# An mLSTM layer and a spectral mixer on one core: the gates of chunk 1 computed apart from those of chunks 2 to 5, and a new order of the steps

## The chip, the cores and the metric

The kernel runs on one core of a Trainium2 chip. Its time is the device time of one execution in microseconds; several executions are timed, and the median counts. TensorE is called PE here (its weight loads PEld), VectorE DVE, ScalarE ACT, GpSimd POOL; SP is the engine whose queue issues nearly all DMAs.

## The reference

Two layers follow one another. The first is an mLSTM: for 4 batches of 8 heads a 40x40 state is updated token by token over 768 tokens, with gates that are kept stable by a running maximum.

```
for t in range(768):
    m_new = max(f[t] + m, i[t])
    C = exp(f[t] + m - m_new) * C + exp(i[t] - m_new) * outer(v[t], k[t])
    n = exp(f[t] + m - m_new) * n + exp(i[t] - m_new) * k[t]
    y[t] = sigmoid(o[t]) * (C @ q[t]) / max(abs(n . q[t]), 1)
    m = m_new
```

The second takes y as x (4 x 768 tokens x 320 channels):

```
theta = x @ w_theta
y = w_tok_r @ (x * cos(theta)) + w_tok_i @ (x * sin(theta))     # over the tokens
u = x + y
out = u + max(u @ w_ch, 0)
```

## The kernel before

**Chunks, units, pairs.** The 768 tokens are cut into six chunks (0 to 5) of 128. A *unit* is one chunk of one batch, so there are 24 units, n = 4 * chunk + batch; units 0 to 3 belong to chunk 0, 4 to 7 to chunk 1. Two units make a *pair*, and the mixer works on pairs: pair 0 is units 0 and 1, pair 1 units 2 and 3, pair 2 units 4 and 5.

**The gates** (gate_part, L186 to L245). The gates of all heads lie in one tile, a row per head, the tokens along it. A scan on DVE gives the running maximum (best, L196). decay (L199 to L207) turns it into the sum of log decays inside each chunk, one scan for each chunk, and a DMA (L177) stores it to g_d in DRAM. POOL subtracts (L215), growth (L210, L211) makes the weights of the inputs, an exponential on ACT (L222) follows, and PE turns the result chunk by chunk (turn, L228), which ACT or DVE copies to bwT (L231). For chunks past 0, leave (L241) and one more exponential (L243) give the decay from the start of a chunk, stored to e_d (L177). In the kernel before this is done once for chunk 0 and once for chunks 1 to 5 together, that is on 640 columns.

**A unit** (unit_loads and attention). SP loads queries and keys (qk, L313), tokens (tok_t, L317), and, from chunk 1 on, two things that the gates stored: dt from g_d, spread over 128 partitions (L322), and eb from e_d in three DMAs (L330), behind the queries q_t (L327). PE makes the scores (L370); ACT takes the exponentials *exps* (L389, eight pieces); POOL's *select* (L393) clears what lies in the future; DVE *weighs* the scores (L399); PE multiplies by the values, *pv* (L406 with the state, L410 without). From chunk 1 on DVE or POOL first *scales the queries* by eb (L484). A denominator (L417 to L424), an output gate (L430, L432) and X (L439) end the unit. *fade* (L444 to L449), *state* (L454), fadeC (L460, L462) and *update* (L468 to L475) carry the state on.

**A pair** (mix_part and mix). PE transposes X (L609); x_hi, x_lo (L621, L625) split it in two parts of fewer bits, and x_acc (L631, L633) adds it to the sums; PE makes *theta* (L647); turns, part and abs (L655 to L671) bring the angle into range; two *sines* on ACT (L674, L675); *times* (L684) multiplies by x; z_hi and z_lo (L687, L690) split the product. Then five *mixing steps* j = 0 to 4 on PE (L549, 12 products each), each gathered by DVE or ACT (L563 to L570). Pair 0 goes through mix_part in two halves, one for each unit.

**Weights.** The token weights of a chunk come in three pieces. SP loads a piece into one of two raw buffers (L773); size, upper, *lower* and hi, lo (L263 to L285) split it. The load of a piece can go out when the lower of the piece two before it is done (wpool has two raw buffers).

**The order.** Every step is added to a plan by `add`, with its engine and its dependences, and gets the next number. The string ORDER then lists all steps in the order in which they are issued, a number and an engine letter each (V is DVE, A is ACT, G is POOL, T is PE, D is a DMA on SP). Each engine and SP's queue follow that order strictly; between engines the waits come from the data. Some steps at the end of the numbering are *fillers* (L870 to L880): with T they run two products of ones on PE, with V they do nothing.

```
t = self.waiting[n]
assert n not in done and eng in (t.alts or t.eng)
t.eng = eng
t.fn()
```

## Time and profile before

| | |
|---|---|
| median of 3 executions | 355.92 us (355.57 to 356.24) |
| the profiled execution's own time | 357.73 us |
| its span, first to last instruction | 356.0 us |
| granted TensorE clock, mean | 0.947 |
| moved by DMA | 61.56 MB in 25164 packets |
| table loads on ACT | 27 of 1.28 us |

The profile is of one execution. It has a page with the busy time of each engine, a coarse picture of the span and the chain of work that ended last, followed back from the end, and answers to questions on the trace: the timeline of an engine, the waits by engine, the busy time in chosen stretches of the span. A timeline row has start and length in us, engine, line of the kernel, operation, output and inputs, the number of instructions merged into it, and in square brackets the idle time of the engine before it with what ended it. PE's steps overlap a little at their ends, so rows of the timeline add up to slightly more than the time that they take in a row.

### The profile page before, as it was taken

The numbers are of one execution on the slowest core, as the hardware profiler recorded it, in microseconds if no ns is written. First come the engines' busy times: TensorE is split into PE (matmuls) and PEld (weight loads), VectorE is DVE, ScalarE is ACT, GpSimd is POOL, SyncE is SP. The second block draws the span as 40 slices with busy tenths as digits, with TensorE's granted clock in tenths as the row PEclk, the third lists the DMA queues.
The fourth block names the chain that finished last, engine by engine and source line by source line (L and its number), as shares of the span: only waits on it lengthen the run. The fifth ranks groups of instructions, "written<-read, shape, count | busy, mean of one in ns | idle before, by whom it ended". The sixth has DMA issues, their size and how long they took to land.

```text
span 356.0 us, 6570 instructions
## 1 busy us (share of the span) xinstructions
PE 325.5 (91%) x2286; PEld 303.9 (85%) x2289; DVE 297.3 (84%) x629; ACT 220.5 (62%) x567; POOL 123.1 (35%) x111
## 2 busy tenths in 40 slices
PE   1487969979899999998999999999999999999995
PEld 1366959859799999997999989999999989998885
DVE  4998699786889998999989998798899998658632
ACT  2989788888979979596585838987850412201000
POOL 1223442323434636247352611614330092702000
PEclk9877676978999999999899999999999999999999
DMA  6965792996886764489627286346630021000155
GB/s 228 395 228 172 226 261 57 302 327 214 244 329 215 243 210 134 152 250 323 203 71 257 79 263 238 121 142 193 228 87 0 2 43 33 1 2 0 46 196 202
DMA packets 25164, 61.56 MB, mean 173 GB/s; under 512 B 3204, under 2 KB 11052, under 8 KB 25132
## 3 DMA queue, kind: packets, MB, share of 16 engines
q1 hardware_dynamic: 23915, 59.84, 51.1%
q0 software_dynamic: 1216, 1.31, 2.0%
q8 instruction: 18, 0.29, 0.3%
q14 instruction: 15, 0.11, 0.1%
HBM read 55.71 MB, written 4.12 MB: 168 GB/s over the span
## 4 chain that ended last, share of the span: by engine, by line
PE 63%; DVE 17%; DMA 12%; ACT 3%; POOL 2%; issue 2%; SPq 2%; DVEq 0%; POOLq 0%
PE pm L549 25%; PE pm L955 10%; PE pm L647 9%; PE ph L410 8%; DMA qk<-in_qk 5%; DMA eb<-e_d 4%; PE sc L370 3%; PE ph L406 3%; DVE acc L563 2%; PE pm L454 2%; DVE dt L399 2%; DMA q_t<-in_q 2%; DMA sg<-in_og 1%; DVE val L271 1%; DVE val L275 1%
## 5 line engine op out<-in xcount | busy, mean ns | idle before, releaser
L549 PE MATMUL pm<-w,z 128*128 128x384 f32 x600 | 112.2, 339 | 0.0
L549 PEld LDWEIGHTS pm<-w,z 128*128 128x128 f32 x600 | 103.4, 188 | 1.4 <-DVE acc L563 0.2
L563 DVE TENSOR_TENSOR acc<-pm,acc 128x384 f32<-128x384 f32 x100 | 52.1, 549 | 10.9 <-PE pm L549 10.6
L389 ACT ACTIVATE dt<-dt,bwT 128x128 f32<-128x128 f32 x160 | 49.0, 391 | 7.7 <-DMA dt<-g_d 7.6
L410 PE MATMUL ph<-tok_t,dt 128*128 128x41 f32 x384 | 49.4, 291 | 0.0
L410 PEld LDWEIGHTS ph<-tok_t,dt 128*128 128x128 f32 x384 | 48.5, 205 | 0.7 <-issue 0.2
L393 POOL TENSOR_SCALAR_AFFINE_SELECT dt<-dt 128x1024 f32<-128x1024 f32 (+1 forms) x26 | 29.3, 1130 | 49.6 <-ACT dt L389 37.5
L647 PE MATMUL pm<-wthp,xs 128*128 128x320 f32 (+1 forms) x216 | 38.3, 352 | 3.2 <-DVE xs L625 3.2
L647 PEld LDWEIGHTS pm<-wthp,xs 128*128 128x128 f32 (+1 forms) x216 | 30.7, 206 | 8.7 <-issue 4.8
L399 DVE TENSOR_TENSOR dt<-sc,dt 128x512 f32<-128x512 f32 x44 | 28.1, 680 | 1.4 <-PE sc L370 1.3
L955 PE MATMUL pm<-u,w 128*128 128x384 f32 (+1 forms) x112 | 28.4, 355 | 0.0
L370 PE MATMUL sc<-qk 64*128 64x128 f32 x352 | 26.5, 292 | 1.8 <-DMA qk<-in_qk 1.8
L370 PEld LDWEIGHTS sc<-qk 64*128 64x128 f32 x352 | 22.2, 193 | 5.2 <-issue 1.6
L690 POOL TENSOR_TENSOR z<-ab,z 128x640 fp32r<-128x640 f32 x8 | 12.8, 1603 | 35.8 <-DVE den L423 21.4
L549 PE MATMUL pm<-wsm,z 128*128 128x384 f32 x120 | 24.6, 359 | 0.0
L967 DVE SCALAR_TENSOR_TENSOR acc<-pm,acc 128x384 f32<-128x384 f32 x20 | 10.8, 555 | 14.5 <-PE pm L955 14.5
L549 PEld LDWEIGHTS pm<-wsm,z 128*128 128x128 f32 x120 | 22.2, 201 | 0.2
L406 PE MATMUL ph<-C,q_t 120*128 120x123 f32 x120 | 17.2, 279 | 5.2 <-DVE X L439 2.7
L406 PEld LDWEIGHTS ph<-C,q_t 120*128 120x128 f32 x120 | 15.4, 191 | 6.8 <-POOL q_t L484 3.0
L955 PEld LDWEIGHTS pm<-u,w 128*128 128x128 f32 (+1 forms) x112 | 17.6, 187 | 3.0 <-issue 3.0
L430 ACT ACTIVATE sg<-sg,den 128x40 f32<-128x40 f32 x72 | 16.7, 314 | 5.0 <-DVE den L424 5.0
L922 ACT CAST u<-acc 128x768 fp32r<-128x768 f32 x4 | 3.2, 834 | 26.4 <-DVE acc L563 21.5
(136 smaller groups left out, 603.8 us busy)
## 6 DMA issues: line engine op xcount, KB each, us to landing
qk<-in_qk SPq DMA_DIRECT2D x24, 512.0 KB
dt<-g_d SPq DMA_DIRECT2D x20, 512.0 KB
raw<-in_wtok SPq DMA_DIRECT2D x18, 512.0 KB
tok_t<-in_tok SPq DMA_DIRECT2D x24, 364.5 KB
sg<-in_og SPq DMA_DIRECT2D x12, 320.0 KB
q_t<-in_q SPq DMA_DIRECT2D x20, 180.0 KB
eb<-e_d SPq DMA_DIRECT2D x60, 60.0 KB
out<-acc SPq DMA_DIRECT2D x5, 384.0 KB
```

Of the source, the lines that this page charges most:

```text
L370: nc.tensor.matmul(u.sc[s][:, hp], u.qk[rows, 1, hp], u.qk[rows, 0, hp], start=True, stop=True)
L389: nc.scalar.activation(u.dt[:, h, :], src, AF.Exp, bias=bwT[:, c, r:r + 1])
L393: nc.gpsimd.affine_select(d, d, pattern=[[0, h1 - h0], [1, P]], compare_op=ALU.is_ge, fill=0.0, base=0, channel_multiplier=-1)
L399: nc.vector.tensor_mul(d2[:, s], u.sc[s], d2[:, s])
L406: nc.tensor.matmul(u.ph[:, gg * 3 * E1:(gg + 1) * 3 * E1], u.q3[:, gg, :], C[b][:, gg, :], start=(gg == 0), stop=False)
L410: nc.tensor.matmul(u.ph[:, h * E1:(h + 1) * E1], u.dt[:, i, :], v1(h, h + 1), start=(c == 0 and i == 0), stop=(i == H - 1))
L430: nc.scalar.mul(u.s3[:, h], u.s3[:, h], u.den[:, h])
L549: nc.tensor.matmul(pm[:, :TH], x.z[:, a, s, j * P:(j + 1) * P], w[x.c][:, b, s, th * TH:(th + 1) * TH], start=(k == 0), stop=(k == last))
L563: nc.vector.tensor_add(a, pm[:, :TH], a)
L647: nc.tensor.matmul(S_.th[b - b0][:, :DM], p.xs[a0:a1, a, k, :], wt5[a0:a1, s, k, :], start=(x == of(b)[0]), stop=(x == of(b)[-1]))
L690: ENG[e].tensor_sub(zv(1, s), trig(s), zv(0, s).bitcast(F32))
L955: nc.tensor.matmul(o.pm[jj][:, :TH], E_.w[s][a0:a1, col:col + P], us[pr, k][a0:a1, a, ts], start=(x == ones[jj][0]), stop=(x == ones[jj][-1]))
```

## The change

gate_part is called twice for the later chunks: once for chunk 1 alone, once for chunks 2 to 5. The second call's scan starts from the end of the first's. Each has its own store to g_d and e_d (the rows of those tensors are now sliced), its own turn and copies, and its own exponentials. unit_loads of a unit now waits for the stores of its own chunk. The list `gone`, which says when the gates' tile may be used for the weights of chunk 2, holds the stores and turns of both calls. The second call has 11 steps, and so has the first, where one call had 13; so there are 9 steps more, and 3 fillers.

All numbers in ORDER from 78 on are therefore 9 higher for the same step as before (12 higher for the last ones, from the fillers on): 114T is theta of the first half of pair 0 and was 105T. 56 to 66 are chunk 1's gates (56 best, 58 decay, 59 store to g_d, 62 turn, 66 store to e_d), 67 to 77 those of chunks 2 to 5 (69 decay, 70 store, 73 turn, 77 store). Other steps, in the new numbers: 144T the mixing step j=1 of pair 0; 118A and 133A the sines of pair 0's halves, 123A the second z_hi and 124V the z_lo behind it; 242V the last lower of chunk 1's weights, 385D the raw load that follows from it, 266D the loads of q_t and eb for unit 5; 268G and 271V unit 5's scaling of the queries and weighing, 272T its pv; 318G unit 6's scaling, 395A and 396G the hi and lo of the last piece of chunk 2's weights, 338G the select of unit 7; 161A the sigmoid of chunk 1's output gates (before, 152A); 319A and 337A the exps of units 6 and 7.

The order is new as a whole, and for many steps so is the engine: DVE, ACT and POOL have 447, 189 and 99 steps before and 437, 199 and 105 after, counting fillers as none. On POOL stand 11 scalings of the queries instead of 7, and 13 times instead of 9. The last call on PE (the channel product of pair 1's middle columns) is the same, and so is the number of products of each kind, except for 8 fillers on PE instead of 5.

```
--- before.py
+++ after.py
@@ -45,55 +45,55 @@
 ORDER = """
-0V 960G 1D 6D 17D 21D 2D 18D 19D 9D 10V 4D 12V 151D 7D 11G 8D 26A 13V 25D 27V 20D 14A 154D 24D 15T 28V 155T 56V 29A
-30A 32A 31V 16A 22T 156A 33V 58V 38A 69A 71A 81A 34V 59D 39V 23T 35A 36A 70G 98A 37V 966T 153D 40V 82T 73V 72G 43A 48D
-5A 57G 75V 986T 976T 44V 152A 84T 41A 74T 60V 3A 85A 158T 42V 76T 83V 157G 99T 49A 169D 66V 77A 87A 78V 45V 165A 89T
-159V 79G 218D 86G 80V 168D 170T 61A 88G 90V 100V 55G 91T 92V 171A 50V 93T 101T 238D 166T 94A 95V 102A 236D 64T 51V 46A
-62T 96V 52A 104V 47G 67A 103V 63A 68D 998V 105T 53V 65A 237D 219A 224D 962V 167V 172G 242A 97V 106V 116T 54G 107V 160T
-117V 220V 108A 109A 173T 256D 161V 221V 162V 222A 230D 110V 239D 163A 118V 113G 174V 120T 223G 255D 225A 164V 111A
-243G 175T 121V 180A 122V 980V 226V 240T 123A 231A 112V 124A 983T 227V 181T 176A 114A 232V 228A 305D 119A 370D 250A
-254D 177V 115V 125V 135T 178V 260A 306D 182V 128G 179V 241V 183T 129V 244V 229G 233V 245T 371A 130V 184A 376D 372V
-257D 186A 138A 251T 137A 234A 185V 261G 258T 126A 246V 136V 310A 324D 247V 323D 127V 131T 373V 235V 382D 304D 248A
-259V 322D 147T 262V 318G 311G 374A 249V 133A 252A 263T 268V 963V 148V 375G 377A 132V 253V 134A 149A 378V 307D 150A
-383A 187T 264A 328A 390D 384V 269T 188A 379V 308T 265V 270A 522D 189V 329G 985T 380A 312V 388D 190A 143T 309G 302D
-191A 266V 381G 267V 271V 313T 385V 523A 192V 394A 524V 326T 408D 139T 314V 406D 525V 325D 315V 330V 395G 316A 389D
-528D 144V 392T 140V 526V 193A 195V 145A 319T 194G 146A 396V 196A 272T 407D 142A 534D 410T 386A 456D 197V 141A 273A
-988V 320V 214T 327V 412A 317V 387G 275V 321V 527G 331T 529A 215V 391D 274V 336A 530V 276T 458D 338A 474D 332V 999V
-216V 989V 971V 333V 217A 531V 334G 337T 277A 393G 198T 335V 535A 457D 339V 413G 462A 278V 409D 536V 397T 532A 964V
-279V 303A 974V 414V 463G 202T 476D 402G 674D 199V 200V 398V 201V 280A 411V 206T 399V 537V 204V 400G 203V 205V 460T
-404A 281V 968V 284V 282A 210T 540D 208V 283G 454D 285A 992V 997V 464V 209A 680D 480A 403T 286V 478T 207V 533G 405V
-401V 340T 459D 212V 415T 538V 211V 213V 675A 481G 341V 420A 990V 343V 539G 293T 342V 542D 416A 558D 676V 344T 482V
-417V 1010V 294V 418G 546A 295V 544T 345V 290T 677V 461V 686D 678A 475D 346V 547G 422A 419V 421T 681A 679G 291V 347A
...
+0V 969G 1D 21D 17D 6D 2D 18D 8D 19D 10V 9D 12V 24D 7D 20D 11G 4D 13V 25D 56V 14A 58V 67V 59D 26A 15T 164T 27V 32A 57G
+28V 33V 29A 30A 16A 22T 31V 60V 38A 34V 90A 35V 93T 39V 36A 78A 37V 91T 40V 94A 69V 48D 43A 41A 80A 107A 23T 44V 70D
+96A 64V 45V 165A 108T 42V 227D 162D 81G 79G 92A 68G 82V 49A 98T 3A 50V 83T 46A 84V 166G 47V 85T 51V 228A 71V 52A 233D
+163D 109A 167T 178D 229V 86A 5A 177D 61A 87V 982T 230V 88A 979T 168V 95G 239D 995T 97G 231A 99V 55G 65A 179T 101V 72A
+174A 89V 53G 100T 75V 180A 232V 54G 110T 102T 189A 111V 113V 62T 76A 975T 103V 247D 112V 246D 234A 104V 66D 1001T 240A
+160D 105G 73T 245D 181G 114T 74V 63V 106V 235V 125T 115A 169T 116V 126A 236V 251A 259V 379D 175T 77D 117V 988V 170V
+127V 265D 182T 171V 237A 264D 252G 118A 190T 183V 238G 129T 172A 119G 249T 130V 122G 191V 998T 131V 176A 173V 241V
+380A 184T 248D 132A 133A 263D 381V 120A 128A 123A 1010T 185A 269A 315D 974T 134V 242V 121V 385D 124V 314D 266D 186V
+144T 382V 187V 383A 391D 250V 243A 188V 384G 135A 253V 147A 192T 319A 260T 277G 146V 254T 137V 981V 193V 270G 138A
+161A 194V 244G 145V 267T 255V 333D 256V 313D 136V 140T 386A 139V 195A 257V 271V 268G 261A 156T 320G 392A 1027V 262V
+143A 258V 142A 316D 337A 387V 272T 331D 141V 388V 393V 531D 317T 332D 389A 273A 327A 196T 989V 274V 394V 157V 390G
+537D 158V 159A 397D 321V 395A 399D 275A 396G 278T 1005V 991V 197V 152T 338G 1031V 198V 279A 276V 318G 199A 280V 335T
+155A 532V 538A 978V 154V 322T 970V 533V 200A 415D 398D 539V 148T 403A 417D 334D 534V 153V 201G 339V 311D 281T 543D
+328T 149V 204G 282A 150V 151V 401T 202A 283V 323A 329A 345G 999V 284V 285T 205A 203V 421A 206V 1019V 1038V 324V 223T
+325V 286A 336V 326V 422G 330V 340T 404G 224V 400D 980V 287V 225A 535A 288A 540V 465D 536V 541A 219T 226A 467D 1030V
+347V 683D 289A 544V 416D 341V 405V 346T 1012V 342V 207T 402V 312A 343V 290V 344V 293G 419T 983V 986V 1023V 220V 209V
+221A 348V 406T 294A 1014V 545V 418D 222A 210A 471A 411V 211T 546V 485D 463D 208V 407V 408V 483D 291V 466D 409V 215T
+689D 295V 547A 413A 976V 212V 292G 423V 214A 213A 412T 420V 349T 484D 997V 410V 472G 469T 414V 350A 542G 218V 217A
+424T 489A 216V 990V 1007V 1036V 473V 429G 684V 352V 490G 302T 551D 351V 468D 479G 1020V 984V 425V 426V 353T 549D 548V
+427A 685V 430T 690V 354A 304V 487T 303V 972V 1008V 1028V 431A 355V 299T 567D 432V 356A 555A 994V 996V 470V 486D 428V
...
@@ -211,12 +211,13 @@
             nc.vector.tensor_add(by(bw[64:P]), by(bw[64:P]), by_G(G[64:P])[:, :, P - 1:P].broadcast_to([64, n, P]))
 
         a = add("V", us, prio, best, [loaded, after])
+        gated.append(len(plan.waiting) - 1)
         warm_after.append(a)
         j = add("G", 2 * us, prio, lambda gi=i_: nc.gpsimd.tensor_sub(gi, gi, m[:, up]), [a])
         a = add("V", 0.3 * n + 2 * us + 0.45 + 0.2 * (c0 > 0), prio, decay, [a])
         decayed = a
         if c0:
-            decayed = load(0.25, prio, lambda: g_d.rearrange("c r t -> r c t"), by_G(G[0:NR]), [a])
+            decayed = load(0.25, prio, lambda: g_d[c0 - 1:c1 - 1].rearrange("c r t -> r c t"), by_G(G[0:NR]), [a])
         w = add("V", 2 * us, prio, growth, [a, j])
         warm_after.extend([a, w])
         x = add("A", us, prio, lambda: nc.scalar.activation(bw[64:P, t], bw[64:P, t], AF.Exp), [w], "exp")
@@ -241,7 +242,7 @@
                 nc.vector.tensor_add(by(E), by_G(G), gs[:, c0:c1].broadcast_to([P, n, P]))
             e = add("V", us, prio, leave, [w])
             e = add("A", us, prio, lambda: nc.scalar.activation(E[:, t], E[:, t], AF.Exp), [e], "exp")
-            return decayed, done, load(0.25 if c0 else 0.05, prio, lambda: e_d.rearrange("c r t -> r c t"), by(E[0:NR]), [e])
+            return decayed, done, load(0.25 if c0 else 0.05, prio, lambda: e_d[c0 - 1:c1 - 1].rearrange("c r t -> r c t"), by(E[0:NR]), [e])
         return a, done
 
 
@@ -249,7 +250,7 @@
 
     halves = []
 
-    warm_after = []
+    gated, warm_after = [], []
 
     def split(hi, lo, raw, n, prio, loaded, after=(), scale=None):
 
@@ -832,9 +833,13 @@
 
     turned, stored = {0: turned0}, {}
 
-    stored[1], done, stored[2] = gate_part(1, NC, 2000 + PAR["grest"], l_gr, A0)
-    for k in range(1, NC):
-        turned[k] = done
+    prior = A0
+    for c0, c1 in ((1, 2), (2, NC)):
+        g_stored, done, e_stored = gate_part(c0, c1, 2000 + PAR["grest"] + c0, l_gr, prior)
+        prior = plan.waiting[gated[-1]]
+        gone.extend([g_stored, *done, e_stored])
+        for k in range(c0, c1):
+            turned[k], stored[k] = done, (g_stored, None, e_stored)
     for x in GROUPS[0][1:]:
         for k in range(3):
             mix_weights(x, k)
@@ -845,13 +850,11 @@
                 for k in range(3):
                     mix_weights(x, k)
         if n > 1:
-            unit_loads(n, () if c == 0 else (stored[1], None, stored[2]),
+            unit_loads(n, () if c == 0 else stored[c],
                        NOW + PAR["du2"] if n == 2 else 1000 * n + PAR["load"])
         attention(n, turned[c], signed[n // 4])
         if n % 2:
             mixer(q)
-        if n == 3:
-            gone.extend([stored[1], *turned[1], stored[2]])
         if n % 4 == 1 and n // 4 < NC - 1:
             k = n // 4 + 1
```

More of the change, by code (lines that the diff above doesn't have):

```diff
@@ L63 @@
-279V 303A 974V 414V 463G 202T 476D 402G 674D 199V 200V 398V 201V 280A 411V 206T 399V 537V 204V 400G 203V 205V 460T
-404A 281V 968V 284V 282A 210T 540D 208V 283G 454D 285A 992V 997V 464V 209A 680D 480A 403T 286V 478T 207V 533G 405V
-401V 340T 459D 212V 415T 538V 211V 213V 675A 481G 341V 420A 990V 343V 539G 293T 342V 542D 416A 558D 676V 344T 482V
-417V 1010V 294V 418G 546A 295V 544T 345V 290T 677V 461V 686D 678A 475D 346V 547G 422A 419V 421T 681A 679G 291V 347A
-299T 292V 348A 682V 424T 301V 465T 470V 488A 548V 349G 300V 352G 423V 425A 562T 466V 687A 477D 426V 472A 287T 683V
@@ new lines @@
+689D 295V 547A 413A 976V 212V 292G 423V 214A 213A 412T 420V 349T 484D 997V 410V 472G 469T 414V 350A 542G 218V 217A
+424T 489A 216V 990V 1007V 1036V 473V 429G 684V 352V 490G 302T 551D 351V 468D 479G 1020V 984V 425V 426V 353T 549D 548V
+427A 685V 430T 690V 354A 304V 487T 303V 972V 1008V 1028V 431A 355V 299T 567D 432V 356A 555A 994V 996V 470V 486D 428V
+308T 686V 301V 687A 300V 556G 357A 491V 433T 474T 691V 358V 480T 1015V 310V 361G 569D 359A 553T 695D 1003V 309V 475A
+476V 296T 362A 985V 557V 488G 434A 477G 481A 435V 571T 360G 436V 1016V 1025V 437T 363V 297V 688G 1029V 478V 482V 497G
@@ new lines @@
+492T 298V 438A 552D 971V 1021V 696V 697V 550D 568D 376T 499A 439V 493V 1004V 698V 440A 494V 498T 441A 1024V 1013V 495V
+370T 554V 618D 699A 617D 496V 442G 573A 619D 1000V 1037V 973V 378V 615D 500V 558T 377V 570D 692V 445V 835D 841D 443V
+367T 446V 559A 563A 992V 372V 574G 371V 565G 305T 464A 369V 444G 368V 564T 560V 575V 700G 581A 373T 566V 447G 306V
+693A 620D 621T 307V 623A 572G 375V 374V 637D 501T 1002V 694V 635D 364T 636D 561V 504V 562V 502A 624G 576T 503V 836A
+365V 1032V 837V 505T 577A 641A 703D 701D 625V 578V 842A 838V 639T 506A 366V 579G 847D 582T 642G 580V 454T 507V 702D
@@ new lines @@
+622G 719D 643V 508A 583A 843V 626T 509A 631V 584V 457T 627A 455V 707A 638D 510V 633V 721D 632T 844V 705T 456V 513G
+634V 839A 460T 459V 649A 704D 708G 977V 458V 840G 709V 769D 448T 514A 511A 1035V 1011V 462V 515G 461V 725A 1022V 1039V
+585T 628V 449V 706G 723T 450V 586A 512G 451T 715A 587V 588V 640G 589T 848V 1009V 629V 726G 630V 1033V 453V 1018V 452V
+849V 644T 590A 591V 850V 522T 592A 771D 651V 787D 645A 593A 646V 647V 650T 767D 524V 525T 523V 720D 648V 594V 597V
+595A 710T 652V 596G 598A 616A 527V 722D 526V 599V 653T 993V 727V 528T 711A 717A 1026V 712V 654A 713G 716T 775A 789D
@@ new lines @@
+770D 714V 773T 724V 718V 728T 655V 656V 776G 793A 609T 735V 855D 772D 529V 729V 530V 851A 777V 794G 657T 853D 788D
+1043D 730V 610V 783G 611V 733V 791T 658A 774G 734T 845A 867D 659V 612T 731V 660A 732V 661A 795V 778T 736V 1006V 613V
+790D 859A 662G 600T 779V 869D 614V 663V 780V 665V 737T 784T 601V 860G 666A 602V 857T 738A 781V 785A 740V 792G 606T
+801A 739V 664G 861V 741T 667G 873A 608V 782V 786V 768A 796T 607V 856D 742A 519T 797V 913D 1034V 798V 911D 743V 854D
+799G 744V 516T 874G 521V 745A 800V 520V 858G 805T 803G 517V 871T 806V 746G 1017V 518V 802T 807V 680T 749G 808V 747V
@@ new lines @@
+750A 875V 809T 917A 751G 681V 804V 748G 862T 810V 846G 682V 987V 852V 603T 863A 927D 811V 870D 812V 813A 668T 914D
+604V 864V 605V 865G 1049D 868D 677T 912D 918G 931A 669V 926D 925D 866V 670V 671T 678V 679V 814V 674T 815A 673V 672V
+872V 817V 876T 1042A 675V 818V 1044A 676V 1045V 758T 877A 928D 878V 816V 879G 761T 759V 1046V 760V 1047A 1055D 880V
+1048G 915T 763V 916G 762V 881T 930V 755T 919V 932G 882A 819V 920T 884V 1050V 883V 929T 921V 757V 756V 885T 922V 933V
+923A 1056A 820T 924V 886A 1051V 1040V 887V 934T 888V 1057V 889A 1058V 826T 935V 821V 1052V 1059A 822V 890G 764T 827V
@@ new lines @@
+893G 891A 828V 823T 936V 894A 765V 892G 1053A 766V 937A 895G 752T 824V 825V 938V 1060V 939T 753V 754V 940A 1041V 1054V
+902T 942V 1062G 941V 896T 903V 904V 899T 898V 897V 1063V 1064G 905T 901V 900V 1061G 908T 906V 907V 1065V 943T 1067V
+1069A 910V 1066G 909V 1071A 829T 1068V 944A 945V 1072V 946A 832T 947A 1070V 831V 1091T 834V 948V 830V 949V 1089T 951V
+1092V 952A 833V 953G 1084T 950G 954T 1085V 1090V 1086V 963T 955V 956V 957T 965V 964V 1073T 958V 1094V 959V 1096V 1097G
+960T 1075V 1074V 1095V 966T 962V 961V 1098V 1099G 1076T 968V 967V 1100V 1102A 1101V 1081T 1078V 1103G 1077V 1080D
@@ L97 @@
+1109T 1083V 1082V 1088D 1079D 1127T 1111V 1110V 1113D 1093D 1112D 1119T 1128V 1104T 1120V 1121V 1122D 1123D 1114T
+1105V 1106V 1107D 1129D 1108D 1087D 1124T 1116V 1115V 1118D 1117D 1125V 1126D
 """.split()
```

29 lines of the change are left out of this document (removed).

## The prediction

> **What bounds the kernel now.** I read the page first: busy time of the engines, then the chain of waits by engine.
>
> ```profile
> PE 325.5 (91%) x2286; PEld 303.9 (85%) x2289; DVE 297.3 (84%) x629; ACT 220.5 (62%) x567; POOL 123.1 (35%) x111
> PE 63%; DVE 17%; DMA 12%; ACT 3%; POOL 2%; issue 2%; SPq 2%; DVEq 0%; POOLq 0%
> ```
>
> PE carries most of the chain that ended last, but 91% is an average over stages, so I cut the span at places where PE's work changes: the first product of the mixing (59.4), a wait (71.7), its end and what follows (84.4), the third call of theta (105.3), the last transposes (288.4). The columns are busy us of PE, PEld, DVE, ACT and POOL with instructions in brackets, then granted clock, DMA share and GB/s.
>
> ```profile
> 0.00:59.40 59.40, 40.05 (x269) 35.20 (x271) 48.62 (x95) 46.74 (x137) 19.07 (x24) 0.77 0.71 228
> 59.40:71.70 12.30, 11.71 (x88) 10.84 (x86) 9.96 (x24) 11.27 (x36) 3.45 (x3) 1.00 0.90 266
> 71.70:84.40 12.70, 10.13 (x63) 9.17 (x64) 8.63 (x22) 9.77 (x29) 3.80 (x4) 0.73 0.80 275
> 84.40:105.30 20.90, 19.61 (x160) 17.83 (x161) 19.10 (x44) 19.21 (x54) 6.96 (x6) 1.00 0.81 271
> 105.30:288.40 183.10, 180.59 (x1343) 172.51 (x1343) 170.14 (x376) 126.69 (x306) 73.58 (x61) 0.99 0.52 169
> ```
>
> From 105.3 on PE idles 2.5 us in 183 and runs at the full clock: PE's own work is the bound there, with DVE close behind (170.14 of 183.10). Before 59.4 PE idles 19.4 us and its clock is 0.77: there DVE and ACT, not PE, decide when the next product may start. Between, PE is nearly always occupied, yet at a lower clock for a while. So a new order can win only ahead of 105.3; behind it, it can chiefly add waits.
>
> **What PE loses between 59.4 and 105.3.** The chain of waits, at the full clock, gives a price for each kind of PE step: theta, score, a mixing step, state, transposes, and the two halves of pv.
>
> ```profile
> 125.40 2.59 PE pm L647 x18
> 127.99 1.09 PE sc L370 x16
> 129.08 2.28 PE pm L549 x12
> 131.36 0.63 PE pm L454 x6
> 134.09 0.55 PE pm L609 x5
> 134.64 0.67 PE ph L406 x6
> 135.30 1.72 PE ph L410 x16
> ```
>
> ```profile
> 59.39 2.33 PE L549 MATMUL pm<-w,z 128*128 128x384 f32 x12
> 74.27 0.90 PE L406 MATMUL ph<-C,q_t 120*128 120x123 f32 x6 [2.67 <-DVE X L439]
> 77.11 4.94 PE L647 MATMUL pm<-wthp,xs 128*128 128x320 f32 x18
> 96.50 1.16 PE L370 MATMUL sc<-qk 64*128 64x128 f32 x16 [1.28 <-DMA qk<-in_qk]
> 105.12 0.80 PE L454 MATMUL pm<-tok_t 128*120 128x123 f32 x6
> 165.97 0.93 PE L406 MATMUL ph<-C,q_t 120*128 120x123 f32 x6 [1.76 <-POOL q_t L484]
> 168.44 3.90 PE L549 MATMUL pm<-wsm,z 128*128 128x384 f32 x12
> ```
>
> From 59.39 to 105.12 stand 6 mixing steps, 4 pv, 5 scores, 2 theta, 3 state and 2 transposes. Rounding a mixing step to 2.2 (the chain's shorter ones are near 2.1): 13.2 + 9.6 + 5.45 + 5.2 + 1.9 + 1.1 = 36.4 us of work in 45.7 us, so 9.3 us are lost. 2.67 and 1.28 are waits; theta at 77.11 took 4.94 where 2.59 is the price, at the half clock that follows the wait. The rest is short waits, the half clock of two neighbours, and steps slightly over price (about 1.3, which I leave in both kernels).
>
> **Part 1: where the first mixing step comes (A).** In the new list, as in the old, step j=1 of pair 0 waits for the second z_hi on ACT and the z_lo on DVE behind it. In the old trace ACT does 40 steps from the first size of chunk 0's weights to that z_hi:
>
> ```profile
> 13.11 0.71 ACT L263 ACTIVATE val<-raw 128x512 f32<-128x512 f32 x1
> 18.78 0.60 ACT L283 ACTIVATE val<-val 128x480 f32<-128x480 f32 x1 [0.96 <-DVE val L275]
> 26.92 1.28 ACT L389 ACT_TABLE_LOAD   x1
> 28.21 1.14 ACT L389 ACTIVATE dt<-pm,bwT 128x128 f32<-128x128 f32 x4
> 42.11 2.44 ACT L389 ACTIVATE dt<-dt,bwT 128x128 f32<-128x128 f32 x8
> 50.80 2.08 ACT L447 ACTIVATE tok_t<-tok_t,bwT 128x40 f32<-128x40 f32 x9
> 55.71 0.18 ACT L417 ACTIVATE den<-ph 128x8 f32<-128x8 f32 x1 [0.53 <-PE ph L410]
> 55.78 0.45 ACT L687 CAST z<-rr 128x320 fp32r<-128x320 f32 x1
> ```
>
> That is 43.1 us, of which seven idles (0.96 the first, 0.53 the last) make 4.95; so 38.2 of work. The new list puts between the same two steps, in addition: exps of unit 2 (2.1), three state updates (0.8 each, an estimate a little above a third of the 2.08 that nine narrower pieces take), an output gate (1.8, eight such pieces), and theta's turns, an x_hi, an x_acc, a weight hi, a weight size and the gate split's extra (four short exponentials for two long ones, +0.4; these six 2.9 by like rows), together 9.2. It takes out a scale, the sigmoid of chunk 1's output gates (1.25), an x_hi, two copies of the transposes and three small ones: 3.9. Work: 43.5. It can start about 0.4 earlier, since the queries of unit 0 and the gates are loaded ahead of the output gates; with no idle it ends at 56.2, with the old idle at 61.2; I take 57.5, nearer to no idle, as more of ACT's steps now stand behind work that is long done. Then 1 us of DVE (in the old trace 3.2, from 56.2 to 59.39): first mixing step at 58.5. **A = -0.9** (ends -3 and +5).
>
> **Part 2: 59.4 to 105.3 (B).** Three things in the old trace made the 2.67 us wait:
>
> ```profile
> 63.27 0.68 DVE L275 SCALAR_TENSOR_TENSOR val<-raw,val 128x512 int32<-128x512 int32 x1
> 64.02 0.33 SPq L773 DMA_DIRECT2D raw<-in_wtok  x1
> 64.89 1.33 SPq L330 DMA_DIRECT2D eb<-e_d  x3
> 71.97 0.56 DVE L484 TENSOR_TENSOR q_t<-q_t,eb 120x384 f32<-120x384 f32 x1 [1.47 <-DMA eb<-e_d]
> 72.44 1.28 DVE L399 TENSOR_TENSOR dt<-sc,dt 128x512 f32<-128x512 f32 x2
> ```
>
> The last lower() of chunk 1's weights (63.27) frees a raw buffer; the load into it (64.02) was waiting at the head of SP's queue; the loads of eb for unit 5 stand right behind it and land 7 us later; the query scaling, the weighing and pv of unit 5 follow. In the new list SP's order is the same (385D, then 314D, 266D), but 242V, that lower(), stands on DVE ahead of unit 4's query scaling and weighing instead of behind them: right behind the products with the second sine (133A, then 134V), which ACT ends 1.3 us ahead of the z_hi, at 56.2. With 0.5 and 0.7 on DVE it is done at 57.4 instead of 63.9; eb lands 6.5 earlier, near 65.4, the scaling is done on POOL at 66.4 and the weighing at 67.7. PE reaches that pv only at 58.5 + 2.2 + 0.55 + 0.63 + 2.39 + 1.09 + 4.4 = 69.8: the wait goes, and its half clock with it.
>
> What is late next is on POOL and ACT:
>
> ```profile
> 70.60 1.09 POOL L393 TENSOR_SCALAR_AFFINE_SELECT dt<-dt 128x1024 f32<-128x1024 f32 x1 [4.52 <-DMA eb<-e_d]
> 72.82 1.29 POOL L285 TENSOR_TENSOR wsm<-val,wsm 128x512 fp32r<-128x512 f32 x1 [1.13 <-ACT wsm L284]
> 81.76 1.00 POOL L484 TENSOR_TENSOR q_t<-q_t,eb 120x384 f32<-120x384 f32 x1 [0.68 <-DMA eb<-e_d]
> ```
>
> (a) POOL scales unit 6's queries (318G) behind 338G, the select of unit 7, and 396G, the lo of chunk 2's last weights, which needs 395A, and that stands on ACT behind three table loads (3.8), three exps (7.3), a sigmoid (1.2), a fade (2.0) and some fifteen short copies (7.1): 57.5 + 21.4 = 78.9, then lo 1.3, select 1.1, scaling 1.0: 82.3. PE is there after 21.3 us of steps, at 79.8: a wait of 2.5 (0 to 5). (b) theta of pair 2 needs an x_hi that ACT does behind the sine of pair 1 and exps of unit 8, two more loads: 78.9 + 11.5, plus 0.8 on DVE = 91.2; PE is there at 82.3 + 6.9 = 89.2: a wait of 2.0 (0 to 5). So 9.3 becomes 4.5 + 1.3 = 5.8: -3.5. The 2.67 and 1.76 waits above were followed by half clock (theta +2.35; the 3.90 mixing step, +1.6), the 1.28 was not; I charge half of 1.6 to each new wait, +1.6. **B = -1.9** (ends -8.0, if neither wait comes, and +3).
>
> Two of ACT's loads in (a) are new: the sigmoid of chunk 1 now splits the exps of units 6 and 7. A load takes 1.28, and the next ACTIVATE starts 0.01 after it (26.92 and 28.21). [...]
>
> [...]
>
> **Part 3: the split itself (C).** One scan, subtractions and additions over five chunks become the same over one and over four, with a second turn, copy, two stores.
>
> ```profile
> 3.47 0.48 DVE L196 TENSOR_TENSOR_SCAN wsm<-g,wsm 128x128 f32<-128x128 f32 x1 [2.54 <-DMA g<-in_gates]
> 9.04 1.55 DVE L196 TENSOR_TENSOR_SCAN wsm<-wsm 128x640 f32<-128x640 f32 x1
> ```
>
> 640 columns cost 1.55 and 128 cost 0.48, so 0.21 of a scan doesn't depend on length; 8 more instructions on DVE cost at most 1.7 us. DVE idles 10.8 us ahead of 59.4, which hides it: C = 0, to +1.7 if that idle is elsewhere. The two added stores on SP cost one issue each (0.33 as the raw load above). The store of chunk 1's decays leaves earlier, but its reader is not what is late in the old chain: no gain. Chunk 2 reads its gates at unit 8, far behind both stores.
>
> **Part 4: from 105.3 on (D).** The products are the same in number, and the last calls are the same channel products, so PE's work is unchanged. POOL scales the queries of 9 units here instead of 6.
>
> ```profile
> PE ph L406 <- POOL q_t L484: 2.4, 2, 1.8
> ```
>
> Six such steps made PE wait 2.4 us, 0.4 each: three more, **D = +1.2** (ends -4, if the 2.5 of idle and the slow step go, and +4).
>
> Sum: -0.9 - 1.9 + 0 + 1.2 = -1.6 us, on the profiled execution's own 357.73. The median, 355.92, is 1.8 lower; I apply the difference there: **354.3 us**. A difference under 0.2% (0.7 us) can't be told from none.
>
> **The rivals.** *Slower: ACT as late as it was.* If ACT keeps the old 4.95 us of idle, the second z_hi ends at 61.2, the first mixing step comes at 62.2, and A is +2.8: 355.92 + 2.8 - 1.9 + 1.2 = **358.0**. It decides from a first mixing step at about 60.8 on. For it: ACT has 5.3 us more to do there, and six steps more for others to make late. Against: the den steps, which waited for PE (the row at 55.71), come later in the new list.
> *Large gain.* Neither wait (a) nor (b) comes: A -0.9, B -8.0, D +1.2 give **348.2**. It needs POOL's and ACT's queues to run 2 us earlier than my sums.
> *No change.* The head gains, and from 105.3 on DVE, 93% busy, gives PE what it needs no earlier than before: **355.9**. Against it: fewer DVE steps in the new list, since more of times and query scaling are on POOL.
>
> **How the numbers follow.** Forecast case (350 to 355.2) 0.42, large gain 0.12, no change 0.16, slower 0.30. Faster is 0.54. The likeliest case's own range is 350 to 355.2; the whole range, 349 to 358.5, leaves out about half of the large gain and a third of the slower case, whose clock may fall as well.
>
> **What would show it.** Right: the first product of L549 at 57 to 60; no wait of pv for eb near 70; theta of pair 1 at 2.6 instead of 4.9; new PE waits ahead of a pv near 80 and theta near 90; 29 table loads for 27; from 105 on PE idle of about 4 to 5 us. Wrong: the first L549 after 61, a clock under 0.9 past 60, or over 8 us of PE idle behind 105.

## The result, and the profile after

The changed kernel takes 350.38 us (median of 4 executions, 349.67 to 350.57), the kernel before 355.75 in the same set (4 executions, 354.59 to 356.24). The ratio is 0.985, with a 95% interval of 0.982 to 0.988. The forecast was 354.3: the direction and the range hold, the size is 5.4 where I said 1.6. Ratios here and below leave out executions over 1.5% above a kernel's fastest, so that they can differ from the quotient of the medians. The profiled execution took 350.47 (span 348.5, mean clock 0.959). It stands at its median, while the old one (357.73) stood 2.0 above its own; so profile against profile shows 7.3.

The page of the changed kernel, the busy time of the engines and the chain by engine:

```profile
PE 324.1 (93%) x2293; PEld 299.2 (86%) x2295; DVE 286.6 (82%) x618; ACT 224.9 (65%) x580; POOL 130.9 (38%) x117
PE 72%; DVE 13%; ACT 6%; DMA 4%; issue 2%; SPq 1%; DVEq 0%
```

DMA fell from 12% of the chain to 4%, PE rose from 63 to 72. The same cuts of the span as in the prediction, changed kernel (busy us of PE, PEld, DVE, ACT, POOL, then granted clock, DMA share, GB/s):

```profile
0.00:59.40 59.40, 43.26 (x278) 34.72 (x280) 48.22 (x106) 47.27 (x144) 17.47 (x24) 0.77 0.76 246
59.40:71.70 12.30, 9.60 (x73) 8.84 (x74) 12.20 (x26) 12.24 (x30) 6.87 (x6) 1.00 0.83 281
71.70:84.40 12.70, 12.50 (x104) 11.29 (x103) 12.25 (x30) 12.67 (x42) 4.62 (x4) 1.00 0.64 220
84.40:105.30 20.90, 19.92 (x147) 18.58 (x148) 20.66 (x45) 19.77 (x42) 8.35 (x6) 1.00 0.89 270
105.30:288.40 183.10, 182.50 (x1369) 174.12 (x1368) 161.30 (x361) 126.87 (x319) 78.47 (x66) 1.00 0.52 168
```

From 59.4 to 84.4 PE idles 2.7 + 0.2 = 2.9 us; in the old kernel it idled 0.6 + 2.6 = 3.2. The idle is nearly the same. What went is the half clock: the old 71.7 to 84.4 ran at 0.73, which is 3.4 us of full clock lost, and the new one runs at 1.00. Behind 105.3 PE idles 0.6 where it idled 2.5, and I had forecast 4 to 5.

PE's timeline, changed kernel, at the places that the prediction named:

```profile
58.56 0.70 PE L550 MATMUL pm<-w,z 128*128 128x384 f32 x2
60.46 2.01 PE L550 MATMUL pm<-w,z 128*128 128x384 f32 x10 [1.20 <-DVE z L691]
...
71.30 2.38 PE L550 MATMUL pm<-w,z 128*128 128x384 f32 x12 [1.32 <-ACT acc L632]
73.87 0.90 PE L407 MATMUL ph<-C,q_t 120*128 120x123 f32 x6 [0.20 <-DVE X L440]
...
77.52 2.86 PE L648 MATMUL pm<-wthp,xs 128*128 128x320 f32 x18
...
84.12 0.93 PE L407 MATMUL ph<-C,q_t 120*128 120x123 f32 x6
...
90.46 0.87 PE L455 MATMUL pm<-tok_t 128*120 128x123 f32 x6 [0.98 <-DVE acc L568]
...
102.24 0.80 PE L455 MATMUL pm<-tok_t 128*120 128x123 f32 x6
...
161.64 0.90 PE L407 MATMUL ph<-C,q_t 120*128 120x123 f32 x6
```

The wait of 2.67 for eb ahead of unit 5's pv is down to 0.20, and theta behind it takes 2.86 instead of 4.94. The idle of that stretch now comes as several smaller waits, of which the rows show 1.20 and 1.32. The row at 102.24 is the state of unit 7, which the old kernel starts at 105.12; by then the new list has done one mixing step more (2.3) and one score less (1.1). At equal work the new kernel is therefore 2.9 + 1.2 = 4.1 ahead there, and 3.2 of the 7.3 come behind it.

One place accounts for about as much as those 3.2. Old kernel, SP's queue and POOL around 160:

```profile
155.49 0.33 SPq L322 DMA_DIRECT2D dt<-g_d  x1
155.91 0.95 SPq L773 DMA_DIRECT2D raw<-in_wtok  x1
156.95 0.39 SPq L327 DMA_DIRECT2D q_t<-in_q  x1
157.44 1.04 SPq L330 DMA_DIRECT2D eb<-e_d  x3
```

```profile
164.91 1.00 POOL L484 TENSOR_TENSOR q_t<-q_t,eb 120x384 f32<-120x384 f32 x1 [1.95 <-DMA q_t<-in_q]
```

POOL stood idle for 1.95 us there: what made PE wait 1.76 at 165.97 was the load, not POOL. The loads of unit 13 stood behind the decays of unit 15, which wait for a buffer until 155.49, and behind a raw load. With the mixing step at half clock behind it (3.90 for 2.28) the place cost 1.76 + 1.62 = 3.4. In the changed kernel SP sends the same loads 8 us earlier, POOL scales at 158.35, and PE starts that pv at 161.64 without a wait (SP, then POOL):

```profile
148.62 0.66 SPq L328 DMA_DIRECT2D q_t<-in_q  x1
```

```profile
68.31 1.02 POOL L485 TENSOR_TENSOR q_t<-q_t,eb 120x384 f32<-120x384 f32 x1
...
83.07 1.00 POOL L485 TENSOR_TENSOR q_t<-q_t,eb 120x384 f32<-120x384 f32 x1
...
158.35 1.00 POOL L485 TENSOR_TENSOR q_t<-q_t,eb 120x384 f32<-120x384 f32 x1 [1.00 <-DMA eb<-e_d]
```

### The profile page after: what moved, and what is told of

It is laid out like the page before. It is cut to its first block, busy times and chain, and to the rows that moved or that the text cites. A ratio compares the mean times of both kernels' runs of the same rounds, so it can differ in the third digit from the quotient of the medians.

```text
span 348.5 us, 6600 instructions
## 1 busy us (share of the span) xinstructions
PE 324.1 (93%) x2293; PEld 299.2 (86%) x2295; DVE 286.6 (82%) x618; ACT 224.9 (65%) x580; POOL 130.9 (38%) x117
## 4 chain that ended last, share of the span: by engine, by line
PE 72%; DVE 13%; ACT 6%; DMA 4%; issue 2%; SPq 1%; DVEq 0%
PE pm L550 32%; PE pm L958 10%; PE ph L411 9%; PE pm L648 8%; PE sc L371 5%; PE ph L407 4%; ACT dt L390 2%; PE pm L455 2%; DMA eb<-e_d 2%; DVE dt L400 2%; DMA z<-in_wth 2%; PE pm L610 2%; DVE val L272 1%; ACT tok_t L448 1%; DVE val L270 1%
## 5 line engine op out<-in xcount | busy, mean ns | idle before, releaser
L394 POOL TENSOR_SCALAR_AFFINE_SELECT dt<-dt 128x1024 f32<-128x1024 f32 (+1 forms) x26 | 27.8, 1075 | 52.6 <-ACT dt L390 46.0
L648 PE MATMUL pm<-wthp,xs 128*128 128x320 f32 (+1 forms) x216 | 35.4, 333 | 0.0
L648 PEld LDWEIGHTS pm<-wthp,xs 128*128 128x128 f32 (+1 forms) x216 | 28.2, 191 | 5.6 <-issue 4.9
L550 PE MATMUL pm<-wsm,z 128*128 128x384 f32 x120 | 22.9, 342 | 0.0
L455 PE MATMUL pm<-tok_t 128*120 128x123 f32 x120 | 18.7, 289 | 3.5 <-ACT tok_t L448 2.5
L448 ACT ACTIVATE tok_t<-tok_t,bwT 128x40 f32<-128x40 f32 x90 | 20.8, 326 | 0.1
L550 PEld LDWEIGHTS pm<-wsm,z 128*128 128x128 f32 x120 | 20.5, 188 | 0.2
L455 PEld LDWEIGHTS pm<-tok_t 128*120 128x120 f32 x120 | 15.8, 190 | 5.4 <-ACT tok_t L448 3.7
L691 POOL TENSOR_TENSOR z<-ab,z 128x640 fp32r<-128x640 f32 x9 | 14.3, 1591 | 16.3 <-ACT z L688 9.8
L685 POOL TENSOR_TENSOR ab<-ab,X 128x640 f32<-128x640 f32 (+1 forms) x6 | 9.0, 1508 | 25.6 <-ACT ab L676 23.2
```

What stands on the lines that cost most here:

```text
L394: nc.gpsimd.affine_select(d, d, pattern=[[0, h1 - h0], [1, P]], compare_op=ALU.is_ge, fill=0.0, base=0, channel_multiplier=-1)
L448: nc.scalar.mul(k4[:, g, j], k4[:, g, j], by[:, g, j:j + 1])
L455: nc.tensor.matmul(u.st_t[:3 * D, gg * 3 * E1:(gg + 1) * 3 * E1], k9()[:, 3 * gg * D:3 * (gg + 1) * D], v1(3 * gg, 3 * gg + 3), start=(gg ...
L550: nc.tensor.matmul(pm[:, :TH], x.z[:, a, s, j * P:(j + 1) * P], w[x.c][:, b, s, th * TH:(th + 1) * TH], start=(k == 0), stop=(k == last))
L648: nc.tensor.matmul(S_.th[b - b0][:, :DM], p.xs[a0:a1, a, k, :], wt5[a0:a1, s, k, :], start=(x == of(b)[0]), stop=(x == of(b)[-1]))
L691: ENG[e].tensor_sub(zv(1, s), trig(s), zv(0, s).bitcast(F32))
```

## The experiments

The theory was: the order in the head (up to about 105) brings most of the gain, by taking away the wait for eb and its half clock; the split itself gives nothing. The rivals: the split brings it; the part behind 105 brings it. Three sets of four kernels were run, each set on a chip of its own. The old kernel's median was 355.27, 355.95 and 355.51 in them. Below, "the state of unit 7" and "the pv of unit 13" are the starts of those steps on PE in the profiled execution:

| kernel | state of unit 7 | pv of unit 13 | span | median | ratio to the old kernel |
|---|---|---|---|---|---|
| before | 105.12 | 165.97 | 356.0 | 355.75 | 1 |
| after | 102.24 | 161.64 | 348.5 | 350.38 | 0.985 (0.982 to 0.988) |
| new head, old rest | 101.71 | 166.75 | 356.1 | 358.12 | 1.010 (1.006 to 1.013) |
| old head, new rest | 103.28 | 166.28 | 354.1 | 356.95 | 1.007 (1.003 to 1.010) |
| unit 13's loads earlier | 103.91 | 162.84 | 351.8 | 354.92 | 1.004 (0.997 to 1.011) |
| unit 5's loads earlier | 103.53 | 163.13 | 351.5 | 352.67 | 0.985 (0.979 to 0.991) |
| both | 101.26 | 160.18 | 350.5 | 351.96 | 0.988 (0.984 to 0.991) |
| lower() earlier | 104.32 | 163.03 | 351.4 | 355.52 | 0.997 (0.993 to 1.000) |
| new kernel, lower() put back | 102.51 | 162.23 | 348.9 | 350.84 | 0.989 (0.985 to 0.993) |
| new kernel again | 100.78 | 160.43 | 347.5 | 349.57 | 0.986 (0.982 to 0.991) |
| gates together | 103.45 | 162.82 | 350.0 | 351.86 | 0.993 (0.990 to 0.996) |
| gates together again | 103.04 | 162.73 | 350.3 | 351.83 | 0.995 (0.992 to 0.998) |
| old list, split alone | 106.04 | 166.35 | 356.2 | 356.81 | 1.004 (1.000 to 1.008) |
| old list, fillers in the wait | 108.29 | 169.60 | 358.4 | 356.92 | 1.002 (0.998 to 1.006) |

One list gives different profiles: up to the state of unit 7 "old head" and "loads of 13" are the old kernel, and come 1.8 and 1.2 earlier than it. A single profile places a wait; it doesn't size a difference of 2 us.

**New head, old rest; old head, new rest.** The list of one kernel up to the state of unit 7, then the steps that are left in the order of the other.

```
-ORDER = new
+ORDER = new[: state of unit 7] + (old without those steps)
...
+ORDER = old[: state of unit 7] + (new without those steps)
```

> The new list up to the state update of unit 7 (103 in the changed kernel's trace), then the old list for all steps that are left. If the gain is made ahead of that point, 351 to 352 (at the same PE work the changed kernel is 4.0 ahead there in the profiles). If it is made behind it, by PE waiting less from 105 on, 354 to 356. Below 350 if the old rest is the better one.

> The old list up to the state update of unit 7 (105 in the old trace), then the new list for all steps that are left; the split is undone. If the gain is made in the head, 354 to 355.7. If it is made behind it, 351 to 353. My forecast had the new rest 1.2 slower than the old one, which would be 356.9 here.

Both came out slower than the old kernel, and the 358.12 of the new head lies outside all that I had expected. The 356.95 of the new rest is what my forecast of that part would give, but not for its reason: PE waits nowhere for POOL behind 105 in that profile. With the new head the lead is there at the state of unit 7 (101.71), but the pv of unit 13 comes 0.8 later than in the old kernel, and the late loads of unit 13 are back. Between them PE waits 1.62 for DVE at 114.46 and 0.82 at 121.21, places where the old kernel has no such wait; I take it that at the seam steps stand behind others that the other list had placed elsewhere. The record gives this execution a mean clock of only 0.916, but its mixing products take 339 ns in the mean, as in the old kernel (339), and the other five executions, with a mean clock of 0.957 to 0.967, took as long (357.10 to 359.13). So the two cannot say which part brings the gain; they say that a lead in the head isn't kept by itself.

**One load moved behind 105, one ahead of it.** Each moves one step on SP's queue of the old kernel: the loads (queries and eb) of unit 13 ahead of the decays of unit 15; those of unit 5 ahead of the raw load that waits for lower().

```
-... 364T 550V 628D 1028V 961V 433V 826D 561D ...
+... 364T 550V 561D 628D 1028V 961V 433V 826D ...
...
-... 130V 184A 376D 372V 257D 186A ...
+... 130V 184A 257D 376D 372V 186A ...
```

> The old kernel with one step moved on SP's queue: the loads of unit 13's queries and eb ahead of the decays of unit 15, which wait until 155.5 for a buffer, and of the first raw weights of chunk 5. In the old trace these loads go out at 156.95 to 158.48 and POOL's scaling waits 1.95 for them, then PE 1.76 at 165.97, then a mixing step runs at half clock (3.90 for 2.28). If this place is what the new rest has over the old one: no wait ahead of pv of unit 13, no half clock there, 3.4 less in the profile from 160 to 172, and 351.9 to 353.5. If POOL's queue, not the load, holds the scaling back, or the time is given back further on: within 0.7 of the old kernel.

> The old kernel with one step moved on SP's queue: the loads of unit 5's queries and eb ahead of the raw load that waits for lower() of chunk 1's last weights (64.02 in the old trace). They can go out at 61.5 instead of 64.4, so eb lands near 69 instead of 71.9. If the wait of 2.67 ahead of pv of unit 5 and its half clock are what the head lost: wait and half clock go, PE is 2.5 to 5 ahead by 84, part of it is given back at later waits for loads, and the time is 352 to 354.5. If another chain is as late (the weighing behind lower() on DVE, the qk loads at 96): within 0.7 of the old kernel.

> The old kernel with both moves on SP's queue, the loads of unit 5 and those of unit 13. If the two places are independent the gains add: 349 to 352, which is the changed kernel's 350.4 without the new order and without the split. If the new order's gain is spread over the list, no more than half of it: 353 to 355.

Unit 13: its profile has neither wait nor half clock at that pv, as expected, but the time isn't measurably better (1.004, 0.997 to 1.011). A likely reason is in the profiles of the other kernels with the old rest: wait and half clock together cost 3.4 in the old kernel, 2.9 with the split alone and 2.6 with the new head, and nothing in two others where nothing was moved there (unit 5's loads, lower()); with the fillers below PE waited there, 1.59, and kept its clock. It is a place where a load comes just in time or just too late. The profiled execution of before was one of the bad ones. If the old executions go as these 6 profiles do, the place costs 1.7 on average, near to the 1.9 between 7.3 and 5.4.

Unit 5: with one moved step on SP the median is 352.67 for 355.95 in the same set. The ratio of 0.985 rests on three executions, 347.36, 352.00 and 352.07, and the other three took up to 358.16, so that the size of the gain is open; by the medians the ratio is 0.991. SP's queue, DVE and PE, unit 5's loads earlier:

```profile
61.58 0.71 SPq L327 DMA_DIRECT2D q_t<-in_q  x1
62.33 1.47 SPq L330 DMA_DIRECT2D eb<-e_d  x3
64.11 0.37 SPq L773 DMA_DIRECT2D raw<-in_wtok  x1
```

```profile
70.87 0.56 DVE L484 TENSOR_TENSOR q_t<-q_t,eb 120x384 f32<-120x384 f32 x1 [0.58 <-DMA eb<-e_d]
```

```profile
73.45 0.90 PE L406 MATMUL ph<-C,q_t 120*128 120x123 f32 x6 [1.41 <-DVE X L439]
...
75.90 2.83 PE L647 MATMUL pm<-wthp,xs 128*128 128x320 f32 x18
...
84.07 0.90 PE L406 MATMUL ph<-C,q_t 120*128 120x123 f32 x6 [0.99 <-DVE X L439]
...
86.62 2.08 PE L370 MATMUL sc<-qk 64*128 64x128 f32 x16
```

The raw load goes out at 64.11 as before (64.02), so it pays nothing. PE waits 1.41 there, and 1.30 with both moves, where it waited 2.67, 2.46 and 2.18 in three kernels that left this place as it was (the old one, the split alone, unit 13's loads). Theta is at full clock; a new wait of 0.99 with a half clock of 3.41 at 86.63 gives some of it back. Both moves together took 351.96, all six executions between 349.2 and 353.0. That lies within the 349 to 352 that I had expected if the gains add, but as the size of neither single gain is known, whether they add stays open. What does stand is that two moved steps on SP, without the new order and without the split, bring 4.0 by the medians, where the changed kernel brings 5.4 in its set.

**lower() earlier.** The lever that the prediction named, alone, in the old list.

```
-... 125V 135T 178V 260A ... 229G 233V 245T ...
+... 125V 135T 233V 178V 260A ... 229G 245T ...
```

> The old kernel with one step moved on DVE: lower() of chunk 1's last weights behind the second product with the sine, ahead of unit 3's output gates and unit 4's scaling and weighing, as in the new list. By the mechanism of my forecast the raw buffer is free at 61.0 instead of 63.95, and the loads of unit 5 behind the raw load go out 2.5 to 3 earlier: wait 2.67 down to 0 to 0.5, its half clock gone, 352.5 to 354.5. If the weighing of unit 4 and the scaling, now 0.7 later, are what PE waits for, no gain or up to 0.7 slower.

0.997 (0.993 to 1.000): at most a small gain. SP, DVE and PE of this kernel:

```profile
59.13 0.38 SPq L773 DMA_DIRECT2D raw<-in_wtok  x1
59.56 0.48 SPq L327 DMA_DIRECT2D q_t<-in_q  x1
```

```profile
69.48 0.56 DVE L484 TENSOR_TENSOR q_t<-q_t,eb 120x384 f32<-120x384 f32 x1 [1.85 <-DMA q_t<-in_q]
```

```profile
71.78 0.90 PE L406 MATMUL ph<-C,q_t 120*128 120x123 f32 x6 [2.54 <-DVE X L439]
74.30 4.94 PE L647 MATMUL pm<-wthp,xs 128*128 128x320 f32 x18
```

The loads went out 4.8 earlier (59.56 for 64.40) but were used only 2.5 earlier (69.48 for 71.97): 9.9 us after their issue, where they had taken 7.6. And this execution as a whole was 2.5 earlier: its first mixing step came at 56.88 for 59.39. Counted from that step the loads went out 2.7 behind it instead of 5.0 and were used at 12.6 in both. With unit 5's loads ahead of the raw load they went out 2.1 behind it and were used at 11.4. In the lower() kernel the raw load, a DMA of 512 KB, still stands ahead of them and was moved forward with them. So wait and half clock stayed. In these profiles the order on SP was the lever, not the lower().

**The same step put back in the new kernel.** lower() of chunk 1's last weights behind unit 4's scaling and weighing.

```
-... 974T 134V 242V 121V 385D ... 135A 253V 147A ...
+... 974T 134V 121V 385D ... 135A 253V 242V 147A ...
```

> The new kernel with the one step put back that my forecast named: lower() of chunk 1's last weights behind unit 4's scaling and weighing, as in the old list. The raw load and, behind it on SP, the loads of unit 5 then go out at about 65 instead of 60.1, so eb is there at 72 to 73 and pv of unit 5 comes at 75 to 76.5 instead of 73.9, with a wait of 1.5 to 2.7 and, where PE idles long enough, half clock behind it: 351.5 to 355. If the head's gain doesn't hang on this step: within 0.7 of the new kernel's own time in this set.

350.84, ratio 0.989 (0.985 to 0.993), beside 349.57 and 0.986 (0.982 to 0.991) for the unaltered kernel of the same set: a difference inside the intervals.

```profile
60.06 2.01 PE L550 MATMUL pm<-w,z 128*128 128x384 f32 x10 [0.59 <-DVE z L691]
...
74.54 0.90 PE L407 MATMUL ph<-C,q_t 120*128 120x123 f32 x6 [0.65 <-DVE X L440]
```

The reverse test is weak: in the new list the lower() of chunk 2's first piece, now the earlier of the two, freed a raw buffer at 61.3, and the loads went out 1.3 late, not 5. It shows two things on the way. Counted from the first product of the mixing step, unit 5's pv comes at 15.8 where it comes at 15.3 and 15.4 in the two profiles of the unaltered kernel, with a wait of 0.65 for 0.20 and 0.31. And the other ten products of that step, which wait for DVE's z_lo, wait 0.59 instead of 1.20 and 1.19 without that lower() in front of it: the move that I counted as a gain also costs.

**The gates together again, and the split alone.** In the new list one gate_part for chunks 1 to 5, its steps at the places of chunks 2 to 5, with the old numbers; and the old list with the two parts side by side, with the new numbers. The first lines of each:

```
-11G 4D 13V 25D 56V 14A 58V 67V 59D 26A 15T 164T 27V 32A 57G
+11G 4D 13V 25D 14A 56V 26A 15T 155T 27V 32A
...
-15T 28V 155T 56V 29A 30A 32A 31V 16A 22T 156A 33V 58V 38A
+15T 28V 164T 56V 67V 29A 30A 32A 31V 16A 22T 165A 33V 58V 69V 38A
```

> The changed kernel's order with the split undone: one scan, one decay, one pair of stores and so on for the gates of chunks 1 to 5, at the places that the gates of chunks 2 to 5 have in the new list; all else stays in its place. If the gain comes from the order of the other work, the time stays with the changed kernel's, 350.4 plus or minus 0.7. If it comes from chunk 1's gates being there early, most of it goes: 353 to 356.

> The old order with the split alone: the gates of chunk 1 and of chunks 2 to 5 as separate steps, side by side at the places of the old single ones. If the split by itself gives nothing, the time is the old one plus 0 to 1.7 (eight more instructions on DVE): 355.7 to 357.4. If the earlier store of chunk 1's decays and the shorter first half carry the gain, 351 to 354.

> The changed kernel, unaltered, beside the others of this set on the same chip. By its first runs 0.985 of the old kernel. If the old kernel's places with late loads go well on this chip, the ratio is nearer to 1 (0.99).

> The changed kernel's order with the gates of chunks 1 to 5 together again, a second time, now beside the changed kernel on the same chip. If the split gives nothing, within 0.7 of the changed kernel; if the 1.5 between 351.86 and 350.38, which were measured in different sets, are real, 1 to 2 slower than it.

In the old list the split alone brings nothing or costs a little: 356.81, ratio 1.004 (1.000 to 1.008). In the new list it does bring something. Together, the gates took 351.86 (0.993, 0.990 to 0.996) and, beside the unaltered new kernel on one chip, 351.83 (0.995, 0.992 to 0.998) against 349.57 (0.986, 0.982 to 0.991). The theory that the split gives nothing falls: in the new list, with the place that it has there, it is worth 2.3 us by the medians of that set. Where they come from shows on ACT. First the new kernel, then the gates together:

```profile
33.06 1.28 ACT L223 ACT_TABLE_LOAD   x1
...
35.27 1.86 ACT L431 ACTIVATE sg<-sg,den 128x40 f32<-128x40 f32 x8 [0.61 <-DVE den L425]
...
38.53 2.08 ACT L448 ACTIVATE tok_t<-tok_t,bwT 128x40 f32<-128x40 f32 x9
```

```profile
35.31 1.86 ACT L430 ACTIVATE sg<-sg,den 128x40 f32<-128x40 f32 x8 [2.48 <-DVE den L424]
...
37.70 1.28 ACT L222 ACT_TABLE_LOAD   x1
...
39.76 2.08 ACT L447 ACTIVATE tok_t<-tok_t,bwT 128x40 f32<-128x40 f32 x9
```

ACT waits for a denominator until 35.3 in both. In the new kernel the exponential of chunk 1's gates stands ahead of that wait, and the table load for it (1.28) falls into time that ACT idles anyway. With the gates together the exponential, and so the load, stands behind the wait, and all that follows on ACT is 1.23 later. DVE's x_lo comes 1.3 later for it, PE waits, and falls to half clock (PE, then the stretch that follows; new kernel, then gates together):

```profile
49.44 1.48 PE L648 MATMUL pm<-wthp,xs 64*128 64x320 f32 x7 [0.23 <-DVE xs L626]
```

```profile
51.15:64.80 13.65, 10.65 (x81) 9.06 (x82) 12.92 (x29) 13.54 (x41) 5.04 (x6) 1.00 0.94 287
```

```profile
50.78 2.31 PE L647 MATMUL pm<-wthp,xs 64*128 64x320 f32 x7 [1.55 <-DVE xs L625]
```

```profile
51.15:64.80 13.65, 13.31 (x55) 11.71 (x56) 12.86 (x29) 12.78 (x35) 4.23 (x5) 0.50 0.76 254
```

Both profiles of the gates together have that half clock: the one shown for 13.7 us, the other with a clock of 0.5 in the slice from 52.5 to 61.3 of its page. Neither of the two of the new kernel has one there (one of them has 6.8 at 40.1 instead, the other 1.00 from 40 to 288). In the old list no table load stands right ahead of the gates' exponential (at 32.97, the last load at 26.92), so the split has nothing to hide there. That the place of the exponential and not the split as such does it is read from the traces only: with the gates together their inputs are ready at 33.3 (row below, DVE), early enough for the same place, and this was not tried.

```profile
31.40 1.92 DVE L211 TENSOR_TENSOR wsm<-wsm 64x640 f32<-64x640 f32 x1
```

**Fillers in the wait.** Four pairs of dummy products ahead of unit 5's pv in the old list, to part the wait from the half clock.

```
-... 133A 252A 263T ...
+... 133A 252A 962T 963T 980T 998T 263T ...
```

> The old kernel with four pairs of dummy products (about 0.4 to 0.6 us each) on PE right ahead of pv of unit 5, in the wait of 2.67 at 71.6 to 74.3; they leave the wait for eb as it is. If the half clock there (theta 4.94 for 2.6, state 1.42 for 0.8) comes from PE's idling, theta takes 2.6 to 2.9, PE is 2.5 to 3.4 ahead by 84, and the time is 352.5 to 354.5. If the half clock has another cause, theta stays at 4 to 5 and the time within 0.7 of the old kernel.

The experiment missed its aim: 356.92, ratio 1.002 (0.998 to 1.006).

```profile
77.44 0.59 PE L878 MATMUL pm<-ones 128*128 128x512 bf16 x1 [5.08 <-DVE acc L567]
```

A filler needs a PSUM bank, and by this row the bank came free when DVE had fetched a product; on DVE that stood behind unit 5's scaling, which waited 2.55 for eb, and the weighing. So the fillers made a wait instead of filling one.

## Why the prediction was right, and where not

The direction and the range held, but partly by luck: of the four terms B had the right place, C was wrong, D had the wrong sign, and errors inside A and B cancelled.

**A (-0.9).** The first product came at 58.56 for the 58.5 forecast. That agreement is luck: it brought only 2 of the step's 12 products, while my sum was for the second z_hi and the z_lo behind it. This z_hi, which I had at 57.5, ended at 59.33 on ACT (changed kernel):

```profile
58.87 0.46 ACT L688 CAST z<-rr 128x320 fp32r<-128x320 f32 x1
```

The "1 us of DVE" behind it held, and the other ten products came at 60.46. By its end the step is 0.75 later than in the old kernel, not 0.9 earlier. In the second profile of the new kernel all this comes 1.45 earlier, and the step ends 0.7 ahead of the old one; so the profiles don't size A.

**B (-1.9).** The place was right: the wait for eb and its half clock went. A and B together measure -4.1 at the state of unit 7 for -2.8, and that includes what the split brings (C). But most steps of B's working failed and cancelled. lower() was done at 60.0, 2.6 later than I said, and I had moved the landing of eb by as much as its issue, while in the kernels with lower() and with unit 5's loads moved the loads, issued 4.8 and 2.8 earlier, were used 2.5 and 1.1 earlier. When eb landed isn't to be seen here: POOL, busy without a break from 63.76, took up the scaling at 68.31 and not at 65.4. PE was at pv of unit 5 not at 69.8 but at 73.87, because z_lo, a PSUM bank behind ACT's new sigmoid (1.32 <-ACT acc) and three DVE steps that took 1.09, 1.14 and 1.37 (last section) held it. So waits (a) and (b) were over when PE came: 0 for 2.5, and 0 for 2.0. (The 0.98 at 90.46 stands ahead of a state update and is for a bank that DVE reads, not for theta's x_hi.) POOL's scaling of unit 6 ended at 84.07, 1.8 later than forecast, and just in time for 84.12. And the 1.6 for the half clock of the new waits was not due, since no half clock came.

**C (0).** Wrong: -2.3. I priced the split's instructions and stores, and looked for the work that hides them, but not for what its exponential brings along on ACT. These 2.3 are a part of the 4.1, not a further gain: at the state of unit 7 the two profiles with the gates together are 2.9 and 3.3 ahead of the old one at equal work, the two of the new kernel 4.1 and 5.5. Without the split, then, A and B come near their forecast of 2.8, by errors that cancel. The condition of the slower rival, a first mixing step behind 60.8, is what the gates together give (61.06 and 61.57). Even so they stay faster than the old kernel: the wait for eb is gone there too (no wait ahead of unit 5's pv in either profile).

**D (+1.2).** Wrong in sign: about -3.2 by the profiles, of which the bad execution of before is a part. I read "PE <- POOL L484" as POOL's price, 0.4 for each scaling; the row counts two waits, and one of them is 1.8. The row of POOL itself said that it idled 1.95, waiting for a load. More scalings on POOL cost PE nothing here: PE idles 0.6 in all from 105.3 to 288.4.

**The offset.** I took the profile of before as a level 1.8 above the median. It was more than that: it held a half clock at 168 that only half of the six profiles with that rest have.

**What is shown, and what isn't.** Shown is that SP's order makes about 1.2 of the wait of 2.67 ahead of unit 5's pv in the old list, and that the split, where it stands in the new list, is worth 2.3. How the rest of the 5.4 divides between the head and the part behind 105 is not shown: the two kernels made of halves failed to part them, and the profiles alone give 3.2 to a place that not every execution loses.

Table loads are 29 for 27, as forecast, of 1.28 each. The load at 33.06 in the second profile of the new kernel is followed by the next step at 34.35, 0.01 behind its end, and the whole delay on ACT with the gates together is 1.23.
